# GpSimd instead of ScalarE and SP issues the stores of narrowed up weights and the zero fills of spare rows in the expert stage

## The chip, the cores and the metric

The kernel runs on one core of a Trainium2 chip. The metric is the device time of one execution in microseconds (us), the median of several runs. The engines are called as in the profile: PE (TensorE), DVE (VectorE), ACT (ScalarE), POOL (GpSimd) and SP (SyncE, which only issues DMAs). Each has its own instruction queue, worked off in order. ACT and SP issue DMAs into hardware queues, POOL into a software queue; all use the same 16 DMA engines.

## The reference

The model is three parts in a row: a gated linear attention, a mixture of eight experts of which each token takes one, and a gated feed-forward (FFN). The change touches the second, and stores and reads data of the third.

```python
x = np.ascontiguousarray(attn_out.transpose(0, 2, 1, 3)).reshape(B * S, H * D)   # 3072 x 320
...
e_idx = np.argmax(logits, axis=1)
...
for e in range(E):
    mask = e_idx == e
    ...
    h = np.maximum(x[mask] @ w1[e], 0.0)          # 320 -> 1024
    ye = h @ w2[e]                                # 1024 -> 320
    out[mask] = gate_w[mask, None] * eom[mask, e, None] * ye
...
xn = x / rms * rms_g
g = xn @ w_gate                                   # 320 -> 1536
silu = g * (1.0 / (1.0 + np.exp(-g)))
val = xn @ w_val
return (silu * val @ w_out).astype(np.float32)
```

## The kernel before, in words

The program has three stages: attention (to about 200 us), the expert stage (`moe`, to about 420 us) and the FFN (`ffn`, to the end). Values are kept as pairs of float16 numbers, a high and a low part.

The router sorts the tokens by expert and pads each expert to whole blocks of 128 rows. The program has 28 blocks (`NJ`) that always run and 3 spare ones, up to `NBLK` = 31, behind a branch (L1258). Block j goes through these steps:

- `gather(j)` (POOL, L1095): an indirect DMA that collects the block's 128 token rows from DRAM into the tile `xg` (2 buffers).
- `xpose(j)` (SP, L1103): a transposing DMA from `xg` to `xt` (2 buffers).
- `up(j)` (PE, L1143): twice 8 matmuls, for the two halves f of the hidden width. Each half is evacuated by a relu on ACT (L1147) and a subtraction on DVE (L1148) into `h`, and then a transposing DMA on SP (L1151) brings `h` into `hT`. PE starts `up(j)` when `xt` has landed.
- `down(j)` (PE, L1175): 24 matmuls, run two blocks later (`LAG` = 2), behind `up(j+2)`.
- `cgather(j)` (POOL, L1087): collects the block's coefficients into `CG`; `evac(j)` (ACT, L1185 to L1187) scales with them and stores the rows to the DRAM tensor `YD`, one block behind `down(j)`.

The loop over j is written in the order in which each engine gets its instructions. In iteration j it writes: `gather(j+2)`, `xpose(j+1)`, the first half of `up(j)`, the steps `tick(j, 0)`, the second half of `up(j)`, in j = 8, 10, 12 the zero fill of a spare block of `YD` (L1231, issued by SP, 128 rows as 3 pieces of 428 bytes each), `cgather(j-1)`, `evac(j-3)`, `down(j-2)`, and the steps `tick(j, 1)`.

Beside the experts, the stage prepares 16 of the FFN's up weights (`ffn_jobs`, 8 tiles f, two halves g). They come as float64 numbers and are narrowed to pairs of float16. A job has six steps: `load` (SP, L1313: 384 KB into a staging tile `stg`, of which there are 4), two steps of integer work on DVE, `high` (ACT, L1328), `low` (DVE, L1335) and `store` (L1341, issued by ACT: 160 KB to the DRAM tensor `UWS`). A table of due times spreads them: job k loads in block 6k//5 + 2, part 1; `high` and `low` run in block 6k//5 + 5, and `store` in block 6k//5 + 6, part 0, ahead of the other steps of that part. Job k+4 takes the staging tile of job k, so its load waits until that store has landed. For k = 0, 5 and 10 load k+4 stands in the same block as store k (blocks 6, 12 and 18). The stored weights are read back into `UW` (L1284) when the FFN begins.

```python
for step, (late, part) in zip(job, ((0, 1), (2, 0), (2, 1), (3, 0), (3, 1), (4, 0))):
    steps = due.setdefault((6 * k // 5 + late, part), [])
    steps.insert(len(steps) * part, step)
...
def tick(j, part):
    for step in due.pop((j - 2, part), []):
        step()
```

Of the kernel before, what the change touches and what calls it, by code (L numbers as in the profile page):

```python
# [74 lines left out]
class Net:  # L75
# [1016 lines left out]
    def gather(self, j, xg=None):  # L1092
        if xg is None:
            xg = self.M0.tile([128, 2 * DX], F16, tag="xg", bufs=2, name="xg")
        self.nc.gpsimd.indirect_dma_start(  # L1095
            out=xg, out_offset=None, in_=self.XD,
            in_offset=bass.IndirectOffsetOnAxis(ap=self.IDX[:, j : j + 1], axis=0),
        )
        self.T[j] = dict(xg=xg)

    def xpose(self, j):
        xt = self.M0.tile([128, 6, 128], F16, tag="xt", bufs=2, name="xt")
        self.nc.sync.dma_start_transpose(out=xt, in_=self.T[j]["xg"])  # L1103
        self.T[j]["xt"] = xt
# [16 lines left out]
    def moe(self):  # L1121
        nc, M, P = self.nc, self.M, self.P
# [4 lines left out]
        def up(j, mid=None):  # L1127
            t = T[j]
            e = nc.tensor.value_load(self.EOFF[0:1, j : j + 1], min_val=0, max_val=NE - 1)
            t["e"] = e  # L1130
            o1 = nc.tensor.snap(e * (5 * F1))
            t["hT"] = []
            if j >= NJ:
                own = spare.bitcast(F16)[:, 0:2048].rearrange("p (f s k c) -> p f s k c", f=2, s=2, k=4)
            for f in range(2):
                h = M.tile([128, 2, 512], F16, tag="h", bufs=3, name="h")
                if j < NJ:
                    hT = M.tile([128, 2, 4, 128], F16, tag="hT", bufs=5, name="hT")
                else:
                    hT = own[:, f]  # L1140
                ps = P.tile([128, 512], F32, tag="up", bufs=4, name="ups")
                for n, (kx, kw) in enumerate(UP):
                    nc.tensor.matmul(  # L1143
                        ps, t["xt"][:, kx], self.W1[:, ds(o1 + (kw * F1 + f * 512), 512)],
                        start=(n == 0), stop=(n == 7),
                    )
                nc.scalar.activation(h[:, 0], ps, AF.Relu)  # L1147
                nc.vector.scalar_tensor_tensor(  # L1148
                    out=h[:, 1], in0=ps, scalar=0.0, in1=h[:, 0], op0=ALU.max, op1=ALU.subtract
                )  # L1150
                nc.sync.dma_start_transpose(  # L1151
                    out=hT.rearrange("p s k c -> p (s k) c"), in_=h.rearrange("p s f -> p (s f)")
                )
                t["hT"].append(hT)
                if f == 0 and mid:
                    mid()

        def down(j, mid={}):
            t = T[j]
            oa = nc.tensor.snap(t["e"] * (2 * KA * DM))  # L1160
            ob = nc.tensor.snap(t["e"] * (2 * KB * DM))
            ps = P.tile([128, 512], F32, tag="dn", bufs=2, name="dps")
            n = 0
            for k in range(8):
                if k in mid:
                    mid[k]()
                if k < KA:
                    W, o, kk, nk = self.W2A, oa, k, KA
                else:
                    W, o, kk, nk = self.W2B, ob, k - KA, KB  # L1170
                hi = W[:, ds(o + kk * DM, DM)]
                lo = W[:, ds(o + (nk + kk) * DM, DM)]
                hT = t["hT"][k // 4]
                for l, r in ((0, hi), (1, hi), (0, lo)):
                    nc.tensor.matmul(ps[:, 0:DM], hT[:, l, k % 4], r, start=(n == 0), stop=(n == 23))  # L1175
                    n += 1
            t["dn"] = ps

        def evac(j):
            ps = T[j]["dn"]  # L1180
            if j not in (NJ - 3, NJ - 1):
                y = self.LG.rearrange("p i e -> p (i e)")[:, 0:YC]
            else:
                y = self.M0.tile([128, DX], F32, tag="xg", bufs=2, name="yl")[:, 0:YC]
            nc.scalar.activation(y[:, 0:DM], ps[:, 0:DM], AF.Copy, scale=self.CG[:, j : j + 1])  # L1185
            nc.scalar.activation(y[:, DM:YC].bitcast(I32), self.TOK[:, j : j + 1], AF.Copy)
            nc.scalar.dma_start(self.YD[128 * j : 128 * j + 128], y)  # L1187
            T.pop(j)
# [11 lines left out]
# [3 lines that stand above are left out]
# [5 lines left out]
        for j in range(NJ):  # L1208
            if 5 <= j + 2 < NJ:
                gather(j + 2)  # L1210
            if 2 <= j and j + 1 < NJ:
                xpose(j + 1)
            up(j, lambda: tick(j, 0) if j else self.xflip(1))
            if j == 0:
                w2[5][1]()
                w2[2][1]()
                scr = lambda: M.tile([128, 2, 512], F16, tag="h", bufs=3, name="scr").rearrange(
                    "p s f -> p (s f)"
                ).bitcast(F32)
            elif j == 1:  # L1220
                w2[7][0]()
                w2[3][1]()
                w2[7][1]()
                self.weigh(scr())
            elif j == 2:
                down(0)
                self.coefs(scr())
                self.order(scr())
            if j in (8, 10, 12):
                b = NJ + (j - 8) // 2  # L1230
                nc.sync.dma_start(  # L1231
                    self.YD[128 * b : 128 * b + 128].rearrange("p (s c) -> p s c", s=3),
                    self.zero.unsqueeze(1).to_broadcast([128, 3, YC // 3]),
                )
            if j == 2:
                self.cgather(0)
            if j >= 2:
                self.cgather(j - 1)
            if j > LAG:
                evac(j - LAG - 1)  # L1240
            if j > LAG:
                down(j - LAG)
            if j == FJ[0]:
                self.fetch(0, first=True)
            elif j == FJ[1]:
                self.squares(0, range(4))
                self.norm1(0)
                self.tokens(0)
            elif j == FJ[2]:
                for m in range(4):  # L1250
                    self.norm2(0, m)
            tick(j, 1)
# [51 lines left out]
    def ffn_jobs(self):  # L1304

        nc = self.nc

        def job(f, g):
            st = {}

            def load():
                t = st["t"] = self.stg().bitcast(I32)
                nc.sync.dma_start(t[:, 0:768], self.i["wu"][f, g].bitcast(I32))  # L1313

            def some(lo, hi):
                def go():
                    if lo == 0:
                        st["v"], st["steps"] = self.narrow(st["t"], 384)
                    for step in st["steps"][lo:hi]:
                        step()  # L1320

                return go

            def high():
                of = st["of"] = st["t"][:, 0:320].bitcast(F16)
                for k in range(3):
                    c = slice(128 * k, 128 * k + 128)
                    nc.scalar.activation(of[:, c], st["v"][:, c], AF.Copy, scale=self.gs[:, k : k + 1])  # L1328

            def low():  # L1330
                v, of = st["v"], st["of"]
                for k in range(3):
                    c, p = slice(128 * k, 128 * k + 128), slice(64 if k == 2 else 0, 128)
                    out = of[p, c] if k == 2 else of[:, 384 + 128 * k : 512 + 128 * k]
                    nc.vector.scalar_tensor_tensor(  # L1335
                        out=out, in0=v[p, c], scalar=self.gs[p, k : k + 1], in1=of[p, c],
                        op0=ALU.mult, op1=ALU.subtract,
                    )

            def store():  # L1340
                nc.scalar.dma_start(self.UWS[f, :, g], st["of"])  # L1341

            return load, some(0, 2), some(2, 5), high, low, store

        return [job(f, g) for f in range(UF) for g in range(2)]
# [335 lines left out]
```

## Time and profile before

| | |
|---|---|
| time, median of 3 runs | 806.57 us (804.85 to 811.94) |
| the profiled execution: its own time | 812.28 us |
| its span, first to last instruction | 810.5 us |
| PE busy | 765.3 us (94%) |
| DVE, ACT, POOL busy | 432.5, 359.1, 363.6 us |
| granted TensorE clock, mean over the span | 0.979 of full speed |
| bytes moved by DMA | 109.21 MB |

A timeline row gives start, duration, engine (with q where it is the engine's queue that issues a DMA), line, operation, output and input by the program's names, how many were merged, and in brackets the idle time of the engine just before, with what ended it. "issue" is time in which the engine waited for nothing that the profile shows.

### The profile page before, as it was taken

What the parts mean: (1) busy time and instruction counts of PE and PEld (TensorE: products, weight loads), DVE (VectorE), ACT (ScalarE), POOL (GpSimd) and SP (SyncE); (2) the same over time, 40 slices, a digit from 0 to 9 for tenths busy, and PEclk for the clock granted to TensorE, in tenths of its full rate; (3) what the DMA queues carried; (4) which work ended last, traced back from release to release, by engine and by line L of the source; (5) the groups of instructions that cost most, each with busy time, mean ns of one, the idle gap of its engine ahead of it and who ended that gap; (6) DMA issues with size and microseconds to landing.
All of it is one profiled execution on the core that took longest, in us unless ns stands there. A gap on an engine that the chain in (4) does not pass through costs nothing. (4 is left out here: it accounts for less than half of the span.)

```text
span 810.5 us, 15423 instructions
## 1 busy us (share of the span) xinstructions
PE 765.3 (94%) x5292; PEld 485.4 (60%) x5294; DVE 432.5 (53%) x894; ACT 359.1 (44%) x777; POOL 363.6 (45%) x439
## 2 busy tenths in 40 slices
PE   8999999998898998999899999999999999999993
PEld 8799998895454554555454444444565566544662
DVE  7568988898756555563214876778622212244010
ACT  4478877772523332332426665654522232233110
POOL 2557877873322232134216875755634232233221
PEclk9799999999899999999999999999999999999998
DMA  6577878864779999999766332232121020000000
GB/s 184 180 239 239 267 233 260 254 208 160 214 142 217 210 245 190 213 219 207 152 119 223 101 81 67 80 74 61 38 72 41 25 64 17 25 0 1 25 17 25
DMA packets 133973, 109.21 MB, mean 135 GB/s; under 512 B 105687, under 2 KB 114527, under 8 KB 133897
## 3 DMA queue, kind: packets, MB, share of 16 engines
q1 hardware_dynamic: 122105, 87.13, 42.8%
q0 software_dynamic: 5408, 13.83, 6.2%
q10 hardware_dynamic: 6384, 7.24, 3.1%
q8 instruction: 48, 0.79, 0.4%
q14 instruction: 28, 0.23, 0.1%
HBM read 67.59 MB, written 16.82 MB: 104 GB/s over the span
## 5 line engine op out<-in xcount | busy, mean ns | idle before, releaser
L1518 PE MATMUL gv<-XT,UW 128*128 128x512 f16 x1152 | 251.5, 381 | 2.0 <-DVE u L1529 2.0
L1518 PEld LDWEIGHTS <-UW 128*128 128x128 f16 x1152 | 113.1, 98 | 138.4 <-issue 4.6
L1528 DVE SCALAR_TENSOR_TENSOR u<-th,gv 128x512 f32<-128x512 f32 x72 | 49.4, 686 | 155.4 <-ACT th L1522 138.1
L1534 POOL TENSOR_TENSOR h<-u,h 128x512 f16<-128x512 f32 x72 | 84.9, 1181 | 105.1 <-ACT h L1533 104.7
L1143 PE MATMUL ups<-W,xt 128*128 x448 | 105.2, 388 | 16.2 <-DMA xt<-xg 11.6
L1551 PE MATMUL do<-DW,h 128*128 128x320 f16 x864 | 118.3, 299 | 0.0
L1551 PEld LDWEIGHTS <-h 128*128 128x128 f16 x864 | 84.5, 98 | 33.8
L1533 ACT ACTIVATE h<-u 128x512 f16<-128x512 f32 x72 | 45.3, 629 | 112.5 <-DVE u L1529 110.7
L1147 ACT ACTIVATE h<-ups 128x512 f16<-128x512 f32 x56 | 33.2, 597 | 124.7 <-PE ups L1143 87.2
L1148 DVE SCALAR_TENSOR_TENSOR h<-ups,h 128x512 f16<-128x512 f32 x56 | 38.4, 691 | 90.7 <-ACT h L1147 63.0
L1143 PEld LDWEIGHTS <-xt 128*128 128x128 f16 x448 | 44.3, 99 | 70.0 <-DMA xt<-xg 14.5
L1175 PEld LDWEIGHTS <-hT 128*128 128x128 f16 x672 | 65.5, 98 | 31.9 <-issue 2.6
L1095 POOL DMA_INDIRECT xg<-XD,IDX x28 | 28.9, 1030 | 106.9 <-DMA xt<-xg 93.8
L1556 POOL DMA_INDIRECT out_dram<-os,TKN x24 | 23.5, 980 | 80.8 <-ACT os L1554 77.3
L1529 DVE SCALAR_TENSOR_TENSOR u<-u,gv 128x512 f32<-128x512 f32 x72 | 49.5, 688 | 15.4 <-PE gv L1518 11.3
L485 PE MATMUL S<-QK 104*128 104x128 f32 x384 | 51.9, 279 | 1.1 <-DMA QK<-in_pqk_dram 1.1
L1175 PE MATMUL dps<-W2A,hT 128*128 x336 | 50.5, 299 | 1.8 <-ACTq L1258 1.8
L485 PEld LDWEIGHTS S<-QK 104*128 104x128 f32 x384 | 50.6, 196 | 2.6 <-issue 1.8
L541 PEld LDWEIGHTS Y<-t,D 128*128 128x128 f32 x352 | 49.2, 192 | 3.4
L541 PE MATMUL Y<-t,D 128*128 128x41 f32 x352 | 51.2, 248 | 0.0
L1175 PE MATMUL dps<-W2B,hT 128*128 x336 | 50.9, 299 | 0.1
L1522 ACT ACTIVATE th<-gv 128x512 f32<-128x512 f32 x72 | 42.3, 588 | 18.0 <-PE gv L1518 16.3
(278 smaller groups left out, 1121.6 us busy)
## 6 DMA issues: line engine op xcount, KB each, us to landing
t<-in_pk_dram SPq DMA_DIRECT2D x22, 484.0 KB
QK<-in_pqk_dram SPq DMA_DIRECT2D x48, 160.0 KB
stg<-in_wu_dram SPq DMA_DIRECT2D x16, 384.0 KB
stg<-in_w_dram SPq DMA_DIRECT2D x9, 640.0 KB
XD<-xr SPq DMA_DIRECT2D x24, 192.0 KB
YD<-LG ACTq DMA_DIRECT2D x26, 160.5 KB
stg<-in_w_dram SPq DMA_DIRECT2D x8, 512.0 KB
wraw<-in_wo_dram SPq DMA_DIRECT2D x12, 320.0 KB
```

Source lines behind the costliest of these rows:

```text
L485: nc.tensor.matmul(ps[:, i * L : (i + 1) * L], t["kz"][:, j, i], t["t1"][:, i], start=True, stop=True)
L541: nc.tensor.matmul(t["Y"][:, hp, 41 * hf : 41 * hf + 41], t["D"][hf][:, hp * L : (hp + 1) * L], t["vv"][:, 4 * hf + hp], start=False, stop ...
L1143: nc.tensor.matmul(ps, t["xt"][:, kx], self.W1[:, ds(o1 + (kw * F1 + f * 512), 512)], start=(n == 0), stop=(n == 7),)
L1148: nc.vector.scalar_tensor_tensor(out=h[:, 1], in0=ps, scalar=0.0, in1=h[:, 0], op0=ALU.max, op1=ALU.subtract)
L1175: nc.tensor.matmul(ps[:, 0:DM], hT[:, l, k % 4], r, start=(n == 0), stop=(n == 23))
L1518: nc.tensor.matmul(ps, UW[:, f, gv, kw], xt[:, :, 3 * hl + kx], start=(a == 0), stop=(a == 7))
L1522: nc.scalar.activation(th, pg, AF.Tanh, scale=0.5 / (XN * WSC))
L1528: nc.vector.scalar_tensor_tensor(out=u, in0=th, scalar=1.0, in1=pg, op0=ALU.add, op1=ALU.mult)
L1529: nc.vector.scalar_tensor_tensor(out=u, in0=u, scalar=1.0 / (XN * WSC) ** 2, in1=pv, op0=ALU.mult, op1=ALU.mult)
L1533: nc.scalar.activation(hh, u, AF.Copy)
L1534: nc.gpsimd.tensor_tensor(hl, u, hh, ALU.subtract)
L1551: nc.tensor.matmul(ps[:, 0:DM], l[:, s], DW[:, f, w], start=(a == 0), stop=(a == 3 * NF - 1))
```

## The change

Two calls are issued by another engine; what they move, and where they stand in the program, stays.

```diff
             if j in (8, 10, 12):
                 b = NJ + (j - 8) // 2
-                nc.sync.dma_start(
+                nc.gpsimd.dma_start(
                     self.YD[128 * b : 128 * b + 128].rearrange("p (s c) -> p s c", s=3),
                     self.zero.unsqueeze(1).to_broadcast([128, 3, YC // 3]),
                 )
...
             def store():
-                nc.scalar.dma_start(self.UWS[f, :, g], st["of"])
+                nc.gpsimd.dma_start(self.UWS[f, :, g], st["of"])
```

SP's queue in blocks 8 and 9 of the kernel before, from the transpose of block 9's token rows on:

```order
L1103 DMA_TRANSPOSE xt<-xg 128x6x128
L1151 DMA_TRANSPOSE hT<-h 128x8x128 x2
L1231 DMA YD<-zero_73 384x1x107
L1313 DMA stg<-in_wu_dram 128x768
L1103 DMA_TRANSPOSE xt<-xg 128x6x128
```

and the same place after the change:

```order
L1103 DMA_TRANSPOSE xt<-xg 128x6x128
L1151 DMA_TRANSPOSE hT<-h 128x8x128 x2
L1313 DMA stg<-in_wu_dram 128x768
L1103 DMA_TRANSPOSE xt<-xg 128x6x128
L1151 DMA_TRANSPOSE hT<-h 128x8x128 x2
```

The zero fill between the second hT transpose and the load of a raw weight is gone from SP; the same holds in blocks 10 and 12.

POOL's queue in blocks 7 to 9 of the kernel before:

```order
L1095 DMA xg<-XD,IDX 128x768
L1087 DMA CG<-CD,IDX 128x1
L1095 DMA xg<-XD,IDX 128x768
L1087 DMA CG<-CD,IDX 128x1
L1095 DMA xg<-XD,IDX 128x768
L1087 DMA CG<-CD,IDX 128x1
```

and after the change, beginning at the same gather:

```order
L1095 DMA xg<-XD,IDX 128x768
L1341 DMA UWS<-stg 128x640
L1087 DMA CG<-CD,IDX 128x1
L1095 DMA xg<-XD,IDX 128x768
L1341 DMA UWS<-stg 128x640
L1231 DMA YD<-zero_73 384x1x107
L1087 DMA CG<-CD,IDX 128x1
L1095 DMA xg<-XD,IDX 128x768
L1341 DMA UWS<-stg 128x640
L1087 DMA CG<-CD,IDX 128x1
```

The store now stands behind the gather of the block after next and ahead of the gather of the coefficients; the zero fill follows the store in blocks 8, 10 and 12. On ACT the store between `high` and the second relu (L1147) of a block is gone, 16 times. PE's and DVE's order does not change.

## Rows read from the trace of the kernel before

**Rows 1.** Busy time by stretches, one per block: us from:to, length, busy (instructions).

```profile
core 0: us, PE busy (x) PEld busy (x) DVE busy (x) ACT busy (x) POOL busy (x), PEclk, DMA share, GB/s
...
276.38:284.23 7.85, 6.88 (x43) 3.91 (x40) 2.82 (x7) 2.57 (x7) 0.00 (x0) 1.00 1.07 202
...
314.65:323.04 8.39, 8.39 (x40) 4.34 (x40) 3.91 (x9) 2.57 (x7) 3.89 (x4) 0.80 0.82 197
...
385.45:396.40 10.95, 7.54 (x42) 3.75 (x40) 3.12 (x7) 4.84 (x15) 2.60 (x6) 1.00 0.79 164
```

**Rows 2.** Waits of PE in the expert stage: us in total, times, longest.

```profile
PE ups L1143 <- DMA xt<-xg: 11.6, 7, 3.2
```

**Rows 3.** Timeline of PE: the up matmuls of blocks 8, 10, 12, 14, 20, 25.

```profile
269.67 3.61 PE L1143 MATMUL ups<-W,xt 128*128 x16 [0.70 <-DMA xt<-xg]
...
284.23 3.61 PE L1143 MATMUL ups<-W,xt 128*128 x16 [0.96 <-DMA xt<-xg]
...
298.41 3.61 PE L1143 MATMUL ups<-W,xt 128*128 x16 [0.59 <-DMA xt<-xg]
...
314.65 5.30 PE L1143 MATMUL ups<-W,xt 128*128 x16 [2.65 <-DMA xt<-xg]
...
358.60 3.61 PE L1143 MATMUL ups<-W,xt 128*128 x16 [1.18 <-DMA xt<-xg]
...
396.40 5.30 PE L1143 MATMUL ups<-W,xt 128*128 x16 [2.29 <-DMA xt<-xg]
```

**Rows 4.** Timeline of SP's queue: xt of block 2, then blocks 6 to 14.

```profile
213.17 1.36 SPq L1103 DMA_TRANSPOSE xt<-xg  x1
...
258.56 3.23 SPq L1151 DMA_TRANSPOSE hT<-h  x2
261.89 0.71 SPq L1313 DMA_DIRECT2D stg<-in_wu_dram  x1
262.70 1.22 SPq L1103 DMA_TRANSPOSE xt<-xg  x1
...
277.59 1.07 SPq L1231 DMA_DIRECT2D YD<-zero  x1
278.71 0.61 SPq L1313 DMA_DIRECT2D stg<-in_wu_dram  x1
...
290.79 0.59 SPq L1231 DMA_DIRECT2D YD<-zero  x1
291.43 0.61 SPq L1313 DMA_DIRECT2D stg<-in_wu_dram  x1
...
298.43 1.22 SPq L1103 DMA_TRANSPOSE xt<-xg  x1
...
305.02 0.59 SPq L1231 DMA_DIRECT2D YD<-zero  x1
305.71 0.59 SPq L1313 DMA_DIRECT2D stg<-in_wu_dram  x1
306.40 1.30 SPq L1103 DMA_TRANSPOSE xt<-xg  x1
```

**Rows 5.** Timeline of POOL: a plain DMA, and gathers of blocks 2, 8 and 15.

```profile
4.93 0.62 POOL L173 DMA_DIRECT2D cst<-in_cst_dram  x1
...
210.00 1.12 POOL L1095 DMA_INDIRECT xg<-XD,IDX  x1 [0.30 <-issue]
...
255.92 0.95 POOL L1095 DMA_INDIRECT xg<-XD,IDX  x1 [4.61 <-DMA xt<-xg]
257.18 0.95 POOL L1087 DMA_INDIRECT CG<-CD,IDX  x1 [0.30 <-issue]
...
303.42 1.03 POOL L1095 DMA_INDIRECT xg<-XD,IDX  x1 [2.20 <-DMA xt<-xg]
```

**Rows 6.** Timeline of ACT: the first store, and a relu with its wait.

```profile
257.22 0.33 ACTq L1341 DMA_DIRECT2D UWS<-stg  x1
...
388.55 0.60 ACT L1147 ACTIVATE h<-ups 128x512 f16<-128x512 f32 x1 [4.32 <-remote]
```

## The prediction

> **What bounds the kernel now.** I read the busy time by stretches first, with the expert stage cut into its blocks of 128 rows. A block is 40 matmuls on TensorE (16 up, 24 down), and undisturbed it takes 6.7 us. The stage runs from 225 to 420 us. In the stretch of one block [rows 1] TensorE is busy 6.88 of 7.85 us and the DMA engines' mean share is 1.07 (packets overlap): both are nearly full, and what TensorE loses is a wait. The list of waits says for what: in the stage 11.6 us in seven waits are for "xt<-xg", the transposed token rows of the next block [rows 2]. The timeline of TensorE [rows 3] shows where: ahead of block 8 (0.70 us), block 10 (0.96), block 12 (0.59), block 14 (2.65), block 20 (1.18), block 25 (2.29), and one at the start that is left aside. Two of them cost more than the wait: after 2.65 and 2.29 us the next 16 matmuls took 5.30 us, where 3.61 is the rule, and the granted clock of that stretch is 0.80 [rows 1, 3]; after 1.18, 0.96 and 0.70 us they took 3.61. So a long wait costs 1.69 us besides itself, a short one does not.
>
> **Why xt is late.** SP issues, in each block j, the transpose of xt for block j+1, the two hT transposes of block j, a zero fill where there is one, and the load of the next raw weight. The second hT transpose can only start when the block's up matmuls are evacuated, so whatever SP issues behind it pushes the next xt transpose. For blocks 10, 12 and 14 that transpose stands behind a zero fill and a load [rows 4], and just these three blocks start with a wait. From its issue to its use or release: with the load alone ahead, 298.43 to 303.42 (POOL's gather is released by the same landing, [rows 5]) is 5.0 us, and 262.70 to 269.67 is 7.0; with zero fill and load ahead, 306.40 to 314.65 is 8.25.
>
> **The change, part by part.** It moves 3 zero fills from SP to POOL and 16 stores from ACT to POOL; nothing else changes on any engine, and PE's and DVE's order is the same.
>
> *Zero fills off SP.* The load behind each starts earlier by the distance of the two issues: 278.71 - 277.59 = 1.12 us, 291.43 - 290.79 = 0.64, 305.71 - 305.02 = 0.69 [rows 4], and so does the xt transpose behind it. That covers the wait of 0.96 ahead of block 10 and that of 0.59 ahead of block 12: 1.55 us. Ahead of block 14 it covers 0.69 of 2.65. In addition the fill's 160.5 KB no longer stand ahead in SP's own DMA queue. What that is worth the trace does not show alone; it is between 0 (the same bytes still pass the same engines) and 8.25 - 5.0 = 3.2 us (all of the excess over the quick case). I take 1.3, nearer to 8.25 - 7.0 = 1.25, since the engines are full there. Then the wait of 2.65 falls to about 0.65, by 2.0 us, and is short enough for the clock to stay: another 1.69. Sum of this part: 1.55 + 2.0 + 1.69 = 5.2 us; at least 1.55 + 0.69 = 2.2, at most 1.55 + 2.65 + 1.69 = 5.9.
>
> *Zero fills on POOL.* Each is 384 rows of 428 bytes. A plain DMA of 124 KB cost POOL 0.62 us early in the program, a gather of 128 rows costs 0.95 [rows 5]; so 0.6 us to 3 x 0.95 = 2.9 us each. Behind it waits the gather of coefficients, which is used two blocks later, and then the next xg gather, which waited 4.61 us for its buffer anyway [rows 5]. Nothing.
>
> *Stores off ACT.* 16 issues of 0.33 us [rows 6]. In the trace ACT waits for TensorE's up results in nearly every block, and hT of block j is used two blocks later: nothing. If that cover were gone it would be 16 x 0.33 = 5.3 us.
>
> *Stores on POOL.* The store stands behind xg's gather and ahead of the coefficients' gather: 255.92 + 1.25 = 257.17 us for the first [rows 5], and ACT issued it at 257.22 [rows 6]. It is as early as before; POOL then spends 0.6 to 1.0 us on it. What is new is that three loads (raw weights 4, 9 and 14, in blocks 6, 12 and 18) take the staging buffer of the store issued in the same block, and SP waits for its landing. In block 6 SP is ready for the load at 258.56 + 3.23 = 261.79 [rows 4], so 257.22 landed within 4.6 us when ACT issued it. From POOL the only unhidden landing in rows is the gather at 210.00, whose transpose SP could issue at 213.17 [rows 4, 5]: 3.2 us, with the engines less busy; and the store now lies behind a gather of 192 KB in POOL's queue. Bounds: no wait (3.2 us), or the 7.0 us that the slower transpose took, 2.4 us too late. I take 0.5 us at each of the three: 1.5 us lost, since xt of blocks 8, 14 and 20 is late already.
>
> A rule of the Trainium skill speaks against this part. DMA: Bandwidth & Descriptors, section Latency and other measured facts, gives the first byte at about 0.6 us for a DMA from SP or ACT and about 1 us from GpSimd. By that alone each store lands 0.4 us later, an estimate of 1.2 us over the three loads. No row here separates the first byte from the landing.
>
> **The sum.** 5.2 - 1.5 = 3.7 us gained. It is made against the profiled execution (812.28 us, span 810.5), which lies 5.7 us over the median of 806.57; the waits should be much the same in the others, so I take it from the median: 806.57 - 3.7 = 802.9 us. The bounds of the terms give 806.57 - 5.9 = 800.7 at the one end and, with 2.2 gained and 3 x 2.4 = 7.2 lost, 811.6 at the other.
>
> **Rivals.** *Only issue time is saved*: the bytes still hold up xt in whichever queue they are. For it: the mean DMA share of 1.07. Against it: 8.25 us with the fill against 5.0 and 7.0 without. Gain 0.96 + 0.59 + 0.69 = 2.2, the clock still drops, and the stores cost nothing: 804.3 us. The Trainium skill holds with this one: DMA: Bandwidth & Descriptors, section Issuing engines are not separate DMA queues, says that DMAs of all engines run on the same 16 and that issuing from several saves only the time to initiate them.
>
> *The store is late for its load* (the other side): POOL's store lands 6.5 us after its issue, 1.9 too late for SP's load in blocks 6, 12 and 18. Block 8 then waits 0.70 + 1.9 = 2.6 and block 20 1.18 + 1.9 = 3.1, both long enough to drop the clock: 2 x (1.9 + 1.69) = 7.2 lost. At block 14 the gain of 3.7 loses 1.9 and the clock's 1.69. So 1.55 + 0.1 - 7.2 = -5.5: 812.1 us. It decides the sign from about 4.6 + 5.2 / 3 = 6.3 us of landing on. For it: the transposes' 5.0 to 8.25 us in this stage. Against it: 3.2 us for the one clean POOL landing.
>
> *The late cluster goes too*: from 385.45 to 396.40 a block takes 10.95 us instead of 6.71, and the next runs at the low clock: 4.24 + 1.69 = 5.9 us [rows 1, 3]. ACT stood there for 4.32 us ahead of a relu, with a releaser that the trace can't name [rows 6]. ACT's program becomes shorter by 16 DMAs, so this may fall elsewhere: 802.9 - 5.9 = 797.0 us. Against it: nothing moved by the change is waited for there.
>
> **How the numbers follow.** The forecast 0.52, only issue time 0.20, the late store 0.13, the late cluster 0.15. About 1% (8 us) is what a measurement of this kernel can tell from no change. Below 798.5 us lies little but the last case: 0.15. Above 814.6 lies the end of the late store: 0.05. Within: 0.80. The range leaves out half of each outer case: 796.5 to 810.5 us; the forecast's own range is 800.7 to 805.5.
>
> **What would show it.** Blocks 10 and 12 start without a wait for xt, block 14 waits under 1.2 us and its 16 up matmuls take 3.61 us. On SP the load follows the second hT transpose directly in blocks 8, 10 and 12. On POOL a store takes 0.6 to 1.0 us and a fill under 2.9, and xg's gather is still released by xt's landing. It is wrong if SP's load in block 6, 12 or 18 starts over 1 us after the second hT transpose is issued, if block 14 still runs at the low clock, or if xt waits appear ahead of blocks that had none.

## The result and the profile after

Side by side, the changed kernel took 799.0 us (median; 794.2 to 808.3) and the kernel before 808.7 us: a ratio of 0.9883, 95% interval 0.9834 to 0.9931. Two further comparisons gave 0.9896 (0.9844 to 0.9948) and 0.9917 (0.9885 to 0.9950). So it gains some 8 us (6.7 to 9.5 by the three ratios). The 799.0 us lie within the stated range of 796.5 to 810.5 us, but below the forecast's own range of 800.7 to 805.5: the gain is 1.8 to 2.6 times the 3.7 us of the sum.

The profiled execution of after took 794.2 us, with a span of 792.4, against 812.3 and 810.5 before. I cut both spans at the first gather of `xg`, the first FFN matmul and the end of the last matmul:

| us | before | after | the kernel before, run once more |
|---|---|---|---|
| attention | 207.3 | 204.9 | 203.1 |
| expert stage | 220.9 | 212.6 | 213.1 |
| FFN | 370.0 | 369.1 | 369.0 |
| last matmul to the end of the span | 12.3 | 5.8 | 12.3 |

The third column is the lesson of this table. An unchanged kernel, profiled again, shows nearly the same 8 us less in the expert stage. The stage of one execution is therefore no measure of the change. The last row is: it stays at 12.3 in the unchanged kernel and falls only in the changed one.

First the places that the prediction named. PE's up matmuls of blocks 10, 11, 12, 14 and 22 of after (start, duration; in brackets the idle time before, with what ended it):

```profile
282.83 3.62 PE L1143 MATMUL ups<-W,xt 128*128 x16
290.27 3.61 PE L1143 MATMUL ups<-W,xt 128*128 x16 [0.57 <-DMA xt<-xg]
296.98 3.62 PE L1143 MATMUL ups<-W,xt 128*128 x16
...
311.49 3.61 PE L1143 MATMUL ups<-W,xt 128*128 x16 [0.92 <-DMA xt<-xg]
...
367.06 3.61 PE L1143 MATMUL ups<-W,xt 128*128 x16 [0.90 <-DMA xt<-xg]
```

Where [rows 3] had waits of 0.96 and 0.59 us there are none, and block 14 waits 0.92 instead of 2.65 us and keeps the full clock (3.61 for 5.30 us). PE's waits for xt in the stage of after (us, times, longest), against 11.6 in 7 [rows 2]:

```profile
PE ups L1143 <- DMA xt<-xg: 6.4, 5, 3.8
```

The longest of these is block 5's, a place that the change doesn't touch. But two signs of being wrong that the prediction named are there as well. Waits for xt appear ahead of blocks that had none: block 11 (0.57 us) and block 22 (0.90). And in the two later profiles of the changed kernel block 12 waits 1.59 and 0.66 us, and block 14 waits 1.49 and 1.28, over the 1.2 that the prediction allowed. One block of after (block 9) by the busy time, to be set beside the first line of [rows 1]:

```profile
core 0: us, PE busy (x) PEld busy (x) DVE busy (x) ACT busy (x) POOL busy (x), PEclk, DMA share, GB/s
...
276.20:282.83 6.63, 6.63 (x41) 3.83 (x40) 2.78 (x6) 2.57 (x7) 1.19 (x2) 1.00 1.20 235
```

PE is busy throughout, with the DMA engines at a mean share of 1.20. SP's queue in blocks 6, 8, 10 and 12 of after (q marks the queue that issues):

```profile
258.51 3.44 SPq L1151 DMA_TRANSPOSE hT<-h  x2
262.04 1.42 SPq L1313 DMA_DIRECT2D stg<-in_wu_dram  x1
...
276.06 0.97 SPq L1313 DMA_DIRECT2D stg<-in_wu_dram  x1
277.13 1.88 SPq L1103 DMA_TRANSPOSE xt<-xg  x1
...
286.11 3.47 SPq L1151 DMA_TRANSPOSE hT<-h  x2
289.67 0.53 SPq L1313 DMA_DIRECT2D stg<-in_wu_dram  x1
...
300.26 3.30 SPq L1151 DMA_TRANSPOSE hT<-h  x2
303.65 0.53 SPq L1313 DMA_DIRECT2D stg<-in_wu_dram  x1
```

The load follows the second hT transpose directly, in block 6 too, where a late store would have held it (258.51 + 3.44 = 261.95, and the load starts at 262.04); it only takes 1.42 us to issue, for 0.71 before [rows 4]. POOL in block 8, and all its stores and fills (duration in ns as min/median/max):

```profile
270.02 0.94 POOL L1095 DMA_INDIRECT xg<-XD,IDX  x1 [5.35 <-DVE stg L1301]
270.96 0.58 POOL L1341 DMA_DIRECT2D UWS<-stg  x1
271.53 0.82 POOL L1231 DMA_DIRECT2D YD<-zero  x1
272.65 1.15 POOL L1087 DMA_INDIRECT CG<-CD,IDX  x1 [0.30 <-DVE h L1148]
```

```profile
L1341 POOL DMA_DIRECT2D UWS<-stg x16: 578/584/607, 254.9 to 380.2; - x16
...
DMA to landing us min/median/max: 2.6/4.5/6.6
```

```profile
L1231 POOL DMA_DIRECT2D YD<-zero x3: 790/797/822, 271.5 to 298.4; - x3
```

Now the end, which no row ahead of the prediction shows. The busy time from the last matmul to the end of the span, before and then after:

```profile
798.20:810.50 12.30, 0.00 (x0) 0.00 (x0) 0.00 (x0) 0.44 (x1) 0.96 (x1) 0.70 0.04 13
```

```profile
786.70:792.40 5.70, 0.00 (x0) 0.00 (x0) 0.00 (x0) 0.44 (x1) 0.96 (x1) 0.83 0.08 29
```

Both hold one ACT instruction and one scatter on POOL, 1.4 us of work in all. The rest is POOL's queue instruction DRAIN, at the line where the program's context closes. The view of that line gives POOL's three DRAINs (ns as min/median/max; the first to start is the long one), before and after:

```profile
L1676 POOLq DRAIN  x3: 46/109/10417, 799.2 to 810.2; - x3
```

```profile
L1676 POOLq DRAIN  x3: 46/109/3891, 787.7 to 792.2; - x3
```

Before, it runs from 799.2 us for 10.42 us; after, for 3.89. That is 6.5 us, the difference of the last row of the table. The packets of the last scatter end while it runs. The rest of it, before and then after, has no engine busy and no byte moved (the last two figures are the DMA share and GB/s):

```profile
801.60:809.60 8.00, 0.00 (x0) 0.00 (x0) 0.00 (x0) 0.00 (x0) 0.00 (x0) 0.60 0.00 0
```

```profile
790.10:791.60 1.50, 0.00 (x0) 0.00 (x0) 0.00 (x0) 0.00 (x0) 0.00 (x0) 0.60 0.00 0
```

### The profile page after: what moved, and what is told of

Its sections match the earlier page's. It is cut to its first block, busy times and chain, and to the rows that moved or that the text cites. A ratio compares the mean times of both kernels' runs of the same rounds, so it can differ in the third digit from the quotient of the medians.

```text
span 792.4 us, 15458 instructions
## 1 busy us (share of the span) xinstructions
PE 758.9 (96%) x5292; PEld 483.0 (61%) x5294; DVE 434.1 (55%) x894; ACT 358.9 (45%) x777; POOL 375.2 (47%) x458
## 3 DMA queue, kind: packets, MB, share of 16 engines
q0 software_dynamic: 6368, 16.94, 7.4%
## 5 line engine op out<-in xcount | busy, mean ns | idle before, releaser
L1147 ACT ACTIVATE h<-ups 128x512 f16<-128x512 f32 x56 | 33.3, 596 | 115.3 <-PE ups L1143 107.8
L1554 ACT ACTIVATE os<-do 128x320 f32<-128x320 f32 x24 | 10.5, 437 | 88.8 <-PE do L1551 80.7
```

## The experiments

In all of these only the named instructions differ from the kernel before (or, where it says so, from the changed kernel). "DRAIN" is the long one of POOL in the profiled execution, "packets" those of POOL's software queue in the table of DMA queues.

| kernel | fills issued by | stores issued by | ratio (95% interval) | DRAIN, us | packets |
|---|---|---|---|---|---|
| before once more | SP | ACT | 0.9998 (0.9958 to 1.0038) | 10.41 | 5408 |
| one more memset | SP | ACT | 1.0040 (1.0001 to 1.0079) | 10.41 | 5408 |
| fills on ACT | ACT | ACT | 0.9987 (0.9944 to 1.0029) | 10.42 | 5408 |
| one more small DMA | SP | ACT | 1.0018 (0.9978 to 1.0058) | 10.50 | 5440 |
| fills only | POOL | ACT | 0.9938 (0.9895 to 0.9980) | 3.24 | 5600 |
| fills early | POOL, at 30 us | ACT | 0.9920 (0.9875 to 0.9965) | 3.24 | 5600 |
| extra fills early | SP, and POOL at 30 us | ACT | 0.9956 (0.9923 to 0.9989) | 3.26 | 5600 |
| stores only | SP | POOL | 0.9935 (0.9897 to 0.9973) | 3.54 | 6176 |
| the change | POOL | POOL | 0.9883, 0.9896, 0.9917 | 3.89 | 6368 |
| fills early, stores on POOL | POOL, at 30 us | POOL | 0.9929 (0.9892 to 0.9965) | 3.90 | 6368 |
| the change and 12 fills | POOL | POOL | 1.0153 (1.0104 to 1.0203) | 6.25 | 7136 |

**The kernel before once more.** No edit.

> The kernel before, once more, to see what differs from execution to execution. Three theories share out the 18.1 us between the two profiled spans (810.5 and 792.4). Queue theory: the stage from the first xg gather to the first FFN matmul is what changed, so here it takes about 221 us again and POOL's last DRAIN and the low clock vary. Clock theory: most of it is time at the low granted clock, so span times (1 - clock) explains the spread of the runs and the rest stays near 793.5 us in every run. End theory: POOL's DRAIN behind the last scatter takes 10.4 us in the kernel before and 3.9 us in the changed one because of the change, so it is 10.4 us here again; by chance, if it is near 4.

The time is the same, and so is the DRAIN (10.41 us), as the theory of the end expected. Its profile is the third column of the first table.

**Fills only.**

```diff
             if j in (8, 10, 12):
                 b = NJ + (j - 8) // 2
-                nc.sync.dma_start(
+                nc.gpsimd.dma_start(
```

> Only the three zero fills go to POOL; the stores stay on ACT. Queue theory: blocks 10 and 12 start without a wait of their own and block 14 waits under 1.2 us, 3 to 6 us faster in the stage, ratio about 0.994. If the stores do it: 1.000. End theory: the DRAIN is short here too if any plain DMA more on POOL does it.

It gains 0.62% (5.0 us), and the DRAIN falls to 3.24 us. In its profile blocks 10 and 12 start without a wait and block 14 waits 1.23 us. So both theories got what they expected, and this kernel can't tell them apart.

**Stores only.**

```diff
             def store():
-                nc.scalar.dma_start(self.UWS[f, :, g], st["of"])
+                nc.gpsimd.dma_start(self.UWS[f, :, g], st["of"])
```

> Only the 16 stores go to POOL; the fills stay on SP. Queue theory: nothing gained in the stage or up to 1.5 us lost at the loads of blocks 6, 12 and 18, ratio 1.000 to 1.002, and the waits ahead of blocks 10, 12 and 14 are there as before. Rival, that ACT's hardware queue held up SP's: the waits at blocks 8, 18 and 20 shrink and the ratio is about 0.993. End theory: the DRAIN tells whether the stores shorten it.

The stores alone, priced at a loss of 1.5 us in the prediction, gain 0.65% (5.2 us), as much as the fills alone (0.62%). Together that would be 1.27%, for 0.8 to 1.2% of the change; the intervals are too wide to tell whether the two add up. The expectation that the waits ahead of blocks 10, 12 and 14 are there as before failed. SP still issues the fills ahead of the loads here, and yet these blocks start so:

```profile
285.83 3.61 PE L1143 MATMUL ups<-W,xt 128*128 x16
...
299.25 3.62 PE L1143 MATMUL ups<-W,xt 128*128 x16
...
314.05 3.61 PE L1143 MATMUL ups<-W,xt 128*128 x16 [1.21 <-DMA xt<-xg]
```

It is one profile, but in it the waits are as short as with the fills on POOL. The rival, that ACT's queue held up SP's, is not settled by it: block 18 has no wait and block 20 waits 0.60 us, but block 8 still waits 1.03. That the part with a predicted loss gains, and by the same amount as the other, speaks against queues in the expert stage as the main cause, and sent me through the rest of the span.

**Fills early.** POOL issues the three fills among its constants, and none is issued in the stage.

```diff
         nc.gpsimd.dma_start(self.CD[NT // 2 : NT // 2 + 1], self.zh[:, 0:2].bitcast(F32))
+        for b in range(NJ, NBLK):
+            nc.gpsimd.dma_start(
+                self.YD[128 * b : 128 * b + 128].rearrange("p (s c) -> p s c", s=3),
+                self.zero.unsqueeze(1).to_broadcast([128, 3, YC // 3]),
+            )
...
-            if j in (8, 10, 12):
+            if j in ():
```

> The three zero fills are issued by POOL at the start of the program (behind the other constants, near 30 us), and none in the expert stage; the stores stay on ACT. The most that freeing SP's queue of the fills can give: if the fills on POOL in the stage cost the DMA engines something, this is faster than the fills moved alone by 0.5 to 2 us; if not, the same.

It gains 0.8%, not clear of the fills only. With the profiles at hand the common feature was the end: DRAIN 3.24, 3.54 and 3.24 us in these three. The next kernels ask what shortens it.

**One more memset** on POOL, a repetition of the one on `one8` (L184), and **one more small DMA** on POOL, a repetition of the 4-byte one into `CD` (L193).

```diff
-        nc.gpsimd.memset(self.one8, 1.0)
+        nc.gpsimd.memset(self.one8, 1.0); nc.gpsimd.memset(self.one8, 1.0)
```

> The kernel before with one POOL instruction more near 26 us (a memset of 128 x 8 that is there already, done twice); no DMA is added and the expert stage is as before. In the kernel before, POOL's DRAIN behind the last scatter took 10.4 us in two profiles; in the fills alone, the stores alone, the early fills and the changed kernel 3.2 to 3.9. If it hangs on how many instructions POOL has, the DRAIN is short here and the ratio is about 0.992 (6.7 us of 807). If it hangs on DMAs issued by POOL, it is 10.4 and the ratio 1.000.

> The kernel before with one plain DMA of 4 bytes more on POOL near 29 us (one that is there already, done twice); the expert stage is as before. End theory by DMAs or by instructions: the DRAIN is 3 to 4 us, ratio about 0.992, though nothing near the fills or the stores has changed. Queue theory alone (all of the gain lies in the stage): the ratio is 1.000.

Neither shortens it, and neither kernel is faster. An instruction more leaves it at 10.41; one small DMA makes it 10.50.

**Fills on ACT.** SP's queue loses the fills as in the change, and POOL's program stays that of before.

```diff
             if j in (8, 10, 12):
                 b = NJ + (j - 8) // 2
-                nc.sync.dma_start(
+                nc.scalar.dma_start(
```

> The three zero fills are issued by ACT, the stores stay on ACT, and POOL's program is exactly that of the kernel before. Queue theory: SP's queue is free of the fills, so 3 to 5 us are gained in the stage, ratio 0.994 to 0.996, with the DRAIN still at 10.4 us. End theory alone: the DRAIN is 10.4 us and the ratio 1.000.

This is the test of the prediction's main term, and the gain of 5.2 us isn't there: 0.13%, 1.0 us, by the interval at most 4.5. DRAIN stays at 10.42. In its profile blocks 10 and 14 still wait 0.54 and 1.63 us.

**The changed kernel again**, two more times.

> The changed kernel once more, for a second profile and more runs: ratio 0.984 to 0.993, DRAIN 3.9 us. Queue theory: the stage is again shorter than in the kernel before by about 4 us once the time at the low clock is taken off both; end theory alone: by nothing.

> The changed kernel once more, for comparison with the extra early fills on the same chip. Theory of the end: DRAIN 3.89 us, ratio 0.988 to 0.994, within 3 us of the kernel with extra early fills. Queue theory with the prediction's own terms: 3.7 us or more faster than the kernel with extra early fills.

Both gain again (0.9896 and 0.9917), with a DRAIN of 3.89 us. Their expert stages took 217.8 and 216.6 us, more than the 213.1 of the unchanged kernel's second profile, so that no shorter stage is to be seen in single executions. In the first of the two SP's load of block 18 does wait for the store of its staging tile; SP's queue there, and its wait (us, times, longest):

```profile
341.57 4.48 SPq L1151 DMA_TRANSPOSE hT<-h  x2
347.40 0.33 SPq L1313 DMA_DIRECT2D stg<-in_wu_dram  x1
```

```profile
SPq L1313 <- DMA UWS<-stg: 1.3, 1, 1.3
```

The store was issued at 339.79 us, 7.6 us ahead of the load. Of the six profiles with stores on POOL three show this wait in block 18 (1.3 us here, 1.2 with the 12 more fills, 0.4 with the stores only), and none shows it in blocks 6 and 12. In the eight with stores on ACT the load of block 18 follows the transposes within 0.12 us. A load that starts over 1 us late in one of these blocks is a sign of being wrong that the prediction named.

**Extra fills early.** The kernel before, with the fills of *fills early* issued besides those of SP. They stand at 29.6 us of the span.

> The kernel before, with three more zero fills of the spare rows that GpSimd issues among its constants near 5 us of the span; SP's fills and ACT's stores in the expert stage stay as they are. Theory of the end (what counts is how much GpSimd's queue has carried when the last DRAIN runs; the fills alone brought it from 10.41 to 3.24 us): the DRAIN takes 3.24 us and the time falls by about 7 us, ratio 0.991 to 0.993, though no queue of the expert stage has changed. Queue theory (the gain comes from SP's and ACT's queues in the expert stage): DRAIN 10.4 us, ratio 1.000.

No instruction of SP, ACT or POOL in the expert stage differs from before. The DRAIN:

```profile
L1676 POOLq DRAIN  x3: 46/109/3257, 802.9 to 806.8; - x3
```

and the up matmuls of blocks 10, 12 and 14, for comparison with [rows 3] and with those of after:

```profile
291.67 3.61 PE L1143 MATMUL ups<-W,xt 128*128 x16 [0.99 <-DMA xt<-xg]
...
306.21 3.61 PE L1143 MATMUL ups<-W,xt 128*128 x16 [0.95 <-DMA xt<-xg]
...
321.81 5.31 PE L1143 MATMUL ups<-W,xt 128*128 x16 [2.01 <-DMA xt<-xg]
```

The stage has its waits of before, low clock included, and the end is 7.1 us shorter (5.2 us after the last matmul). The time falls by 0.44%, 3.6 us, by the interval between 0.9 and 6.2. So the end alone makes the kernel faster with the stage untouched. But the 7.1 us lie outside the interval, and the time shows only half of them. In the profile the attention is late by at least the missing part. POOL's `ctmp` product that followed the fills was not late (38.47 us, for 38.89 before), but the next two were: 51.84 us for 47.77, and 61.42 for 55.05. The busy time from 40 to 55 us, before and then here (the figure ahead of the last two is the granted clock, 0.50 being the lower level of 1.2 GHz):

```profile
40.00:55.00 15.00, 15.00 (x158) 13.46 (x157) 9.98 (x27) 11.36 (x24) 5.27 (x8) 0.93 0.71 224
```

```profile
40.00:55.00 15.00, 14.84 (x88) 12.51 (x86) 6.31 (x18) 6.12 (x14) 3.16 (x5) 0.50 0.52 160
```

PE did 88 matmuls at the low clock for 158. In the ten profiles without fills at 30 us it did 158 to 171 there, at a clock of 0.93 to 1.00; the other two with the three fills at 30 us have 99 at 0.66 and 150 at 0.86. So the early fills seem to have a price of their own (the last `ctmp` product is 6.4 us late); that is argued from one profile each, and how it comes about no run here shows. Measured beside it, the change (0.9917) is 0.4%, some 3 us, faster than this kernel, with the two intervals overlapping. That lies between the two expectations (within 3 us by the theory of the end, 3.7 us or more by that of the queues) and decides for neither.

**Fills early, stores on POOL**, which I thought might beat the change.

> The fills issued by GpSimd among its constants instead of in the expert stage, and the stores by GpSimd as in the change: the queue has carried the same as in the changed kernel. Theory of the end: DRAIN 3.9 us, ratio 0.988 to 0.994, no better than the changed kernel. Queue theory: the fills' bytes leave the full stretch of the stage as well, another 1 to 2 us, ratio 0.986 to 0.988.

It doesn't: 0.9929 against 0.9917. The DRAIN is as long as that of the change (3.90 us). Since its fills stand at 30 us too, it doesn't isolate the expert stage.

**The change and 12 fills**, issued at the place of the extra ones, four for each spare block.

> The changed kernel with twelve more zero fills that GpSimd issues among its constants near 5 us of the span. If the DRAIN rises slowly with what the queue has carried (0.12 us for each of the first three fills, estimate from 3.24 in the kernel with fills only and 3.54 to 3.89 with the stores): 3.89 + 12 x 0.12 = 5.3 us, and the end 1.4 us later than in the changed kernel. If it depends only on having passed a point once: 3.9 us. If the point comes again: about 10 us. Whether twelve fills near the start delay the attention is read from the time to the first gather; 12 x 0.8 us of GpSimd would be 9.6 us if all of it lay on the path.

DRAIN:

```profile
L1676 POOLq DRAIN  x3: 46/109/6250, 814.5 to 821.4; - x3
```

It is neither 3.9 nor 10 us: it rises again, by 2.36 us for 12 fills, faster than the first three fills let expect. The kernel is slower for another reason: repeated fills of a block wait for one another, and POOL's work for the attention stands behind them.

```profile
36.88 0.71 POOL L193 DMA_DIRECT2D YD<-zero  x1 [4.87 <-DMA YD<-zero]
...
46.27 0.71 POOL L193 DMA_DIRECT2D YD<-zero  x1 [6.36 <-DMA YD<-zero]
...
54.48 2.19 POOL L193 DMA_DIRECT2D YD<-zero  x3 [5.85 <-DMA YD<-zero]
```

These waits sum to 17.9 us, a cost of my experiment and not of the DRAIN.

**The stage over all profiles.** One execution decides nothing in the stage, but 14 were profiled, and they fall into groups. From the starts of the up matmuls on PE's timeline (us, means; a block of 6.7 us is undisturbed):

| | blocks 8 to 16 | 16 to 24 | 24 to 25 | wait ahead of block 14 |
|---|---|---|---|---|
| fills on SP, stores on ACT (5 profiles) | 58.6 (56.8 to 60.1) | 55.3 (53.7 to 57.9) | 9.2 (7.4 to 11.0) | 2.1 (1.9 to 2.7) |
| the change (3) | 56.6 (55.5 to 58.0) | 57.9 (55.5 to 60.7) | 7.2 (6.7 to 7.7) | 1.2 (0.9 to 1.5) |
| all with fills off SP (8) | 56.0 (54.1 to 58.0) | 57.8 (54.7 to 60.7) | 7.3 (6.7 to 8.0) | 1.0 (0 to 1.6) |

Ahead of block 14 the groups don't overlap, and block 14 ran at the low clock in three of the five profiles of the first row and in none of the eight of the last. Between blocks 16 and 24 the means turn round: 2.4 us longer with the fills off SP (the ranges overlap), and 58.1 us in the six profiles with stores on POOL. *Stores only* has 55.6, 57.7 and 7.7 us in the three stretches and 1.2 ahead of block 14: it goes with the last row, though its fills are on SP. *Fills on ACT*, whose fills are off SP and whose POOL does what it did before, has 57.3, 54.7, 8.0 and 1.6, between the rows or with the first. So the groups show that the early blocks got shorter, and not that the fills on SP were the reason.

## Why the prediction held, and for another reason

The time lay in the range and the sign was right; the cause that I gave isn't the main one. That it came out in the range is luck: most of the gain lies at a place that no term of the sum touches.

**What bounds the kernel now: incomplete.** I read the expert stage closely and never accounted for the 12.3 us after the last matmul, in which no engine does anything but 1.4 us. One row of busy time over the last 12 us would have shown it. No term of the sum touches the place that gave 6.5 us. That moved DMAs shorten the DRAIN is shown: it is 10.4 to 10.5 us in all five profiles with at most 5440 packets on POOL's queue, and 3.2 to 3.9 in all with 5600 to 6368, wherever the added DMAs stand and whatever they carry. How it comes about is open.

**Fills off SP (5.2 us): right in direction, half in size, and not isolated.** The order on SP is what I said, and the waits behind it got shorter; but *stores only* has them as short with the fills on SP, so that the mechanism is argued, not shown. In the groups the waits ahead of blocks 10 and 12 sum to 0.98 us with fills on SP and 0.40 without, a gain of 0.6 for the 1.55 I had taken from one execution. Ahead of block 14 the gain is 1.0 us (2.08 to 1.04) for 2.0; the clock drops there in three of five executions, worth 3/5 x 1.69 = 1.0 us for 1.69. Together 2.6 us, which is what blocks 8 to 16 show (58.6 - 56.0). The mis-sized term is the 5.2, because the profile of before was one of the worse executions: the four other profiles with the same stage have 1.9 to 2.0 us ahead of block 14. *Fills on ACT* bounds the whole at 4.5 us. The 1.69 us rest on the rule that a long wait drops the clock and a short one doesn't. It fails in the profile that it was read from, at the wait that I left aside, ahead of block 5, the longest of [rows 2]:

```profile
248.51 3.61 PE L1143 MATMUL ups<-W,xt 128*128 x16 [3.17 <-DMA xt<-xg]
```

Its matmuls took 3.61 us after 3.17 us of waiting. Ahead of block 14 waits of 1.86 and 1.90 us kept the clock in two profiles and waits of 1.97 and 2.01 lost it in two others, and the change kept it after 2.34 us ahead of block 19. The length of the wait alone doesn't decide.

**Fills on POOL, stores off ACT (nothing): the first held, the second is open.** Fills took 0.79 to 0.82 us, inside the bounds of 0.6 and 2.9. No view isolates a gain from ACT's shorter queue, and *stores only*, with its short waits, doesn't exclude one.

**Stores on POOL (1.5 us lost): at one of the three places, the cost not shown.** Stores took 0.58 to 0.61 us, landing within 2.6 to 6.6 in the first profile. The loads in blocks 6 and 12 did not wait for them; that in block 18 did in three of six profiles, by 0.4 to 1.3 us, where I took 0.5 at each of the three. A loss from the stores, if there was one, lies between blocks 16 and 24: 58.1 us with stores on POOL for 55.3 with all as before. PE's waits for xt there sum to 2.5 us in the mean of the six profiles for 0.8 in the five. But two kernels with stores on ACT and fills on POOL have 56.8 and 59.8 us there, so this is not settled. The rule of the Trainium skill that I set against this part (DMA: Bandwidth & Descriptors, section Latency and other measured facts: a later first byte from GpSimd) could cost nothing where no load waited; whether it is part of the wait in block 18 no run here shows.

**The rivals.** *Only issue time is saved* (2.2 us) is nearest in size to what the stage shows: from block 8 to 25 the five profiles with the stage of before sum to 58.6 + 55.3 + 9.2 = 123.1 us, the three of the change to 56.6 + 57.9 + 7.2 = 121.7, 1.4 us less. Single profiles span 119.0 to 126.7 and 117.8 to 125.8 us, so that these means don't establish it, and the low clock at block 14, which this rival keeps, is in none of the three. The rule that it goes with (the Trainium skill, DMA: Bandwidth & Descriptors, section Issuing engines are not separate DMA queues: issuing from several engines saves only the time to initiate) is not contradicted by 1.4 us, and not tested by it either. *The late store* did not come in blocks 6 and 12. It came in block 18, by over 1 us in two of six profiles; block 20 then waited 0.41 and 1.78 us and kept the full clock, so its price of 3.6 us a block is not there. *The late cluster goes too*: block 24 to 25 takes 7.2 us instead of 9.2 in the mean, but an unchanged stage (*one more memset*) has 7.4 and *fills on ACT*, with three DMAs more on ACT, has 8.0. Whether the change did it stays open.

**The new sum.** End 6.5, stage 1.4 (the three stretches above): 7.9 us, for 6.7 to 9.5 measured. The stage's part rests on means over few executions that differ by more than that, and is argued, not shown; at the least it is nothing, since 6.5 us (0.8%) alone lies in all three intervals of the change.

## What to carry to other kernels

Before pricing a change, account for the whole span, the stretch after the last matmul included; a DMA moved to POOL can change the time of its DRAIN there, in either direction. Profile the unchanged kernel a second time before sizing a wait: here one wait of 2.65 us was 1.9 in most other executions, and a whole stage differed by 8 us with no change at all. In a stage where PE and the DMA engines are both nearly full, look at more than the block that should gain: here blocks 8 to 16 were 2.6 us shorter in the mean and blocks 16 to 24 2.4 longer, though single executions differ by more. And an experiment that moves work out of the stage can pay elsewhere: look there too, as at the attention with the fills at 30 us.

## What was unexpected of the hardware

POOL's DRAIN at the end doesn't grow evenly with what its queue has carried. In packets of that queue: 10.41 us at 5408, 10.50 at 5440, then 3.24 at 5600, 3.54 at 6176, 3.89 at 6368 and 6.25 at 7136. The lines of the queue in the page of before, of *fills only* and of the one with 12 more fills (packets, MB, share):

```profile
q0 software_dynamic: 5408, 13.83, 6.2%
```

```profile
q0 software_dynamic: 5600, 14.32, 6.2%
```

```profile
q0 software_dynamic: 7136, 18.92, 8.3%
```

The value repeats to 0.02 us between kernels with the same number, with the DMAs at 30 us or at 290. A count that starts anew somewhere between 5440 and 5600 would fit, but that is a guess: whether packets, bytes or DMAs count, and what the DRAIN does while no byte moves (8.0 us of it before, 1.5 after), no run here shows.
